# Another order of block 0, totals one step later and later weights of slot 1 in an attention and mixture kernel

## The chip, the cores and the metric

The kernel runs on one core of a Trainium2 chip. The metric is the device time of one execution in microseconds, lower being better, and the number compared is the median of several executions. The core has five engines with a queue each: TensorE (PE in the rows, its weight loads PEld), VectorE (DVE), ScalarE (ACT), GpSimd (POOL) and SyncE (SP). An engine works its queue off in order; engines wait for one another through semaphores.

## The reference

Three layers follow one another, all in float32.

1. Attention with decay over 4 batches, 8 heads, 768 positions, 48 values a head: `y[t] = r[t] · (state + (u k[t]) v[t]ᵀ)`, then `state = w[t] state + k[t] v[t]ᵀ`.
2. A dense layer on the 3072 tokens of width 384: `h = x @ w_in`, `g = max(h, 0) + alpha * min(h, 0)`, `x = g @ w_out`, with 2048 hidden values.
3. Eight experts of 1024 hidden values. Each token goes to the one whose normalised embedding is nearest: `expert_idx = argmax(xn @ en.T / tau)`, `out = gate * (relu(x @ w1[e]) @ w2[e])`, where gate is the chosen expert's softmax probability.

## The kernel before

Tokens are cut into 24 tiles of 128 and those into 8 blocks of 3 tiles. Products in float32 are made of three single-pass products of high and low parts, so most operands exist as a pair: xh and xl, win0h and win0l, gh and gl. ScalarE writes the high part with a copy that rounds, VectorE subtracts it to get the low one.

For block j the dense layer runs 16 f-steps of 128 hidden values. One step has nine matmuls l1 (L458) into h_ps, ScalarE's m (L468, alpha times h), VectorE's min (L472), ScalarE's gh (L478), VectorE's gl (L483), and two steps later nine matmuls l2 (L493) into o_ps.

Block 0 also has to make the attention of its tiles and of those to come, and to convert w_in and w_out to high and low parts. This is issued from the table PLAN, a list of single-engine pieces written in the order in which they enter the queues. `0D.2` is attention part 0 of tile 2 on VectorE, `2P.2` part 2 on TensorE (transposes of k, L345), `2A.2` its copy on ScalarE (L348). 3P (L356) makes the scores, 4P y, 5P the transposes of y (L414) that 5A and 5D turn into xh and xl; 9P (L372) and 9A carry the state, 8A (L297) measures the decay. `cQ.C` is quarter Q of the conversion of weight slab C. `p0P.G`, `p0A.G`, `p1P.G`, `p1A.G` fold the expert embeddings into w_out: p0P (L247) transposes into PSUM, p0A (L252, L253) copies this to wt, p1P (L261) multiplies, p1A (L268, L269) writes s_wp and wout0h. `l.f`, `m.f`, `n.f`, `h.f`, `d.f` and `o.f` are l1, m, min, gh, gl and l2 of step f, and `w.N` is N warm-up matmuls (L444) whose results are not read. 28 more warm-ups run ahead of PLAN. Most PSUM tiles of the attention and of p0P and p1P come from one pool, ps_a, of three buffers; a piece on TensorE that takes one waits until ScalarE or VectorE has emptied the tile that had it.

Behind PLAN the loop over T walks the f-steps of all blocks; `step(k)` moves background generators forward, up to k yields each, and stops at a yield that says WAIT. route(j) (L514 on) computes expert, gate and position of each token of block j. early_table and early_loads, started when block 6 has been routed, compute which experts the first four slots of 256 tokens have and load their weights and rows: `pump` issues w_load (L779, indirect DMAs to raw buffers; there are four of one kind and two of another), `gather` (L811) fetches rows to xg. last_table, started when block 7 has its carry (L559, the tokens counted so far by expert), computes the other slots. Its first act is totals: two small matmuls (L602, L603) that sum carry over partitions and a copy (L605, s_tot).

Then the loop over U walks the slots. A step f of a slot has nine matmuls l3 (L834), ScalarE's g2h (L838), VectorE's g2l (L839) and, two steps later, l4 (L861) with w1h and w1l. Raw weights become high and low parts by split (L790 on ScalarE, L791 on VectorE), 768 columns at a time; split(0, 4) is the first piece of slot 0's second matrix, which l4 of its step 0 reads. EARLY lists the steps of T at which slot 0's splits and transposes run ahead of U.

Of the kernel before, what the change touches and what calls it, by code (L numbers as in the profile page):

```python
# [42 lines left out]
WAIT, DONE, DONE_T = 1, 2, 3  # L43
# [22 lines left out]
AD = (0, 1, 3, 4, 5)  # L66
WARM0 = 28
WPD = (2, 3)
EARLY = [(0, 0, -5), (0, 1, -5), (0, 2, -4), (0, 3, -3), (1, 0, -1), (1, 1, -1), (0, 4, 0)]
SA = 1  # L70
SB = 2
OOB = 1 << 20
# [6 lines left out]

LOADS = [(0, "w"), (0, "rk"), "id", "v", (0, "n"), "e", (1, "w"), (1, "rk"), (1, "n"), (2, "w"), (2, "rk"), (2, "n"), 0, 1, 2, 3, "u"]  # L80
PLAN = """
0D.0 1D.0 8A.0 6D.0 3P.0 3A.0 0D.1 sD 7P.0 7A.0 w.2 1D.1 2P.0 w.8 2A.0 4P.0 6D.1 w.2 c0.0 7P.1 sA 3P.1 0D.2 w.1 4D.0 c1.0 w.8 3A.1
7A.1 c0.1 5P.0 w.2 7P.2 c0.2 7A.2 4P.1 1D.2 5A.0 w.4 c1.1 6D.2 5D.0 w.7 w.3 w.4 c2.0 3P.2 7D.2 c0.3 4D.1 c2.1 3A.2 5P.1 w.4 5A.1
c3.0 c1.2 p0P.0 8A.1 w.2 c2.2 4P.2 5D.1 p0A.0 c1.3 9P.0 eP w.2 8A.2 4D.2 2P.1 9A.0 eA c3.2 5P.2 c0.4 c3.1 2A.1 w.6 w.6 5A.2 5D.2
l.0 c1.4 9P.1 p1P.0 c2.3 m.0 9A.1 c2.4 p1A.0 0D.3 p0P.1 2P.2 2A.2 p0A.1 n.0 c3.4 c0.6 l.1 c0.5 h.0 c3.3 c1.6 7P.3 d.0 c1.5 l.2
7A.3 o.0 m.1 p1P.1 m.2 2P.3 9P.2 c2.6 c0.8 2A.3 p1A.1 c2.5 p0P.2 n.1 c3.6 1D.3 h.1 c0.7 l.3 9A.2 n.2 c3.5 d.1 6D.3 h.2 c1.8 p0A.2
m.3 l.4 9P.3 n.3 o.1 9A.3 l.5 3P.3 8A.3 c2.8 h.3 c1.7 p1P.2 d.2 c0.9 c2.7 d.3 o.2 3A.3 c0.10 c3.8 0D.4 m.5 m.4 n.4 p0P.3 p1A.2
p0A.3 h.4 o.3 c3.7 7P.4 n.5 c1.10 h.5 d.4 4P.3 l.6 7A.4 c2.10 m.6 c0.12 l.7 4D.3 p1P.3 p1A.3 1D.4 d.5 5P.3 5A.3 c3.10 n.6 o.4 m.7
5D.3 h.6 6D.4 d.6 l.8 n.7 0D.5 o.5 c0.11 h.7 m.8 3P.4 7P.5 3A.4 n.8 h.8 c0.14 l.9 7A.5 c1.12 o.6 2P.4 d.7 8A.4 c1.14 m.9 c1.9 o.7
l.10 2A.4 c2.14 d.8 c2.9 c2.12 n.9 p0P.4 c3.9 p0A.4 l.11 m.10 1D.5 p1P.4 h.9 c1.11 8A.5 c3.12 n.10 p1A.4 d.9 4P.4 o.8 l.12 h.10  # L90
4D.4 6D.5 2P.5 c0.13 m.11 p0P.5 d.10 2A.5 5P.4 n.11 c1.13 m.12 c2.11 p0A.5 c3.11 5A.4 o.9 h.11 n.12 c3.14 5D.4 p1P.5 h.12 d.11
p1A.5 l.13 p0P.6 p0A.6 l.14 d.12 m.13 o.10 3P.5 o.11 n.13 c2.13 c0.15 p1P.6 c1.15 m.14 3A.5 h.13 n.14 d.13 h.14 c3.13 l.15 4P.5
m.15 p1A.6 c2.15 4D.5 d.14 p0P.7 o.12 5P.5 p0A.7 p1P.7 5A.5 p1A.7 c3.15 o.13 5D.5 n.15
"""

AT1 = {1: [0, 4, 8], 2: [0, 4, 8]}
# [8 lines left out]
def idx(ap):  # L105
    return bass.IndirectOffsetOnAxis(ap=ap.bitcast(U32), axis=0)
# [3 lines left out]
def tile_main(ctx, tc, keep, x2d, tbl, att, w_in, w_out, alpha, u_row, u_col, emb, tau, w1, w2, cst, out):  # L110
# [125 lines left out]
    def once(nm, shape, dt=F32):  # L236
        return small(nm, shape, dt, 1)
# [362 lines left out]
    def totals(j, ok):  # L600
        tp = ps_a.tile([128, NE + 1, 1], F32, tag="a", name="tot_ps")
        PE.matmul(out=tp[:, 0:NE, 0], lhsT=oneb, rhs=carry[(j + 1) % 2], start=True, stop=True)  # L602
        PE.matmul(out=tp[:, NE:, 0], lhsT=oneb, rhs=ok, start=True, stop=True)  # L603
        tot = once("tot", [128, NE + 1, 1])
        DVE.tensor_copy(out=tot, in_=tp)  # L605
        return tot
# [89 lines left out]

    def last_table():

        tot = totals(NB - 1, okb)
        yield  # L700
        b = above(tot, thr_blk, "nb")
# [2 lines left out]
        n, cu, first = work[:, 0:4 * NE], work[:, 4 * NE:8 * NE], work[:, 8 * NE:12 * NE + 1]  # L704
# [33 lines left out]
        q, h, o, a = (once(f"t{i}", [128, NS1]) for i in range(1, 5))  # L738
# [20 lines left out]
        w = once("t6", [128, 3])  # L759
# [148 lines left out]
    if True:  # L908
# [117 lines left out]
        def pump(most=8, of=(0, 1)):  # L1026
            for i in of:
                while most and queue[i] and busy[i] < (NSG, 2)[i] and queue[i][0][0] < state["known"]:
                    w_load(*queue[i].pop(0))
                    busy[i] += 1  # L1030
                    most -= 1
# [9 lines left out]
        def early_loads():  # L1041
            while state["placed"] < NB - 2:
                yield WAIT
            pump(2)
            for s in range(len(xg)):
                ids_load(s)
            yield
            for i in (1, 0):
                pump(1, (i,))
            yield  # L1050
            for s in range(len(xg)):
                for t in range(2):
                    gather(s, t)
                yield
                if s == 0:
                    pump()
            for s in range(len(xg), ES):
                ids_load(s)

# [14 lines left out]
        for T in range(16 * NB + 2):  # L1074
# [35 lines left out]
            if 32 <= T < 32 + NTILE:  # L1110
                SP.dma_start(out=out[(T - 32) * CH:(T - 31) * CH, :], in_=zero)
            for fn, i, at in EARLY:
                if T - 16 * NB == at:
# [6 lines left out]
        def at(U, fn, *a):  # L1120
            act.setdefault(U, []).append((fn, a))

        for s, k in enumerate(KIND):
            U0, before = FIRST[s], KIND[s - 1]
            at(U0 + (3 if k == "S" else 9), o_scale, s)
            if k != "S":
                for i in range(0 if s else 1, 4):
                    at(U0 + i, split, s, 4 + i)
            else:
                for i in range(2):  # L1130
                    at(U0 + i, relu_single, s, i)
            if s and before != "S":
                for n, i in enumerate((4, 5, 6, 7) if k != "S" else (2, 3, 4, 5, 5, 6, 6, 7)):
                    at(U0 - 8 + i, split, s, n)
            elif s:
                for n in range(4):
                    at(U0 - 2 + (n >= SB), late if n >= SA else split, s, n)
            if s:
                X = U0 - 4 if before != "S" else U0 - 2
                for t in range(NTOK[s]):  # L1140
                    at(X + t, x_T, s, t)
                if s >= ES:
                    at(X - (7 if s == ES else 9), ids_load, s)
# [322 lines left out]
```

## Time and profile before

| what | value |
|---|---|
| median of three executions | 805.33 us (802.21 to 806.11) |
| profiled execution, its own time | 800.48 us |
| its span, first to last instruction | 798.7 us |
| TensorE busy, weight loads busy | 777.0 us, 735.3 us |
| VectorE, ScalarE, GpSimd busy | 545.3, 409.4, 272.2 us |
| mean granted clock of TensorE | 0.994 |
| warm-up matmuls | 89 |

Busy times are sums over the span. Matmuls overlap in the array, and the profile draws each as long as it is under way, so TensorE's sum says little of how full it is. What an edit is worth is read in the stretch where it lies: block 0 ends at some 110 us, the dense layer at some 555 us, and the slots fill the rest.

### The profile page before, as it was taken

The page shows a single profiled execution, that of the slowest core. Times are in us where ns is not written, and L with a number is a line of the kernel's source. Part 1 is how long each engine was busy: PE and PEld are TensorE (multiplying, and loading weights), DVE is VectorE, ACT ScalarE, POOL GpSimd, SP SyncE. Part 2 cuts the span into 40 slices and gives each one's busy share as a digit, 9 for nine tenths or more (in the row PEclk, how much of TensorE's full clock was granted, in tenths as well). Part 3 has the DMA queues.
Part 4 walks back from the last instruction along what each step waited for, and adds up shares of the span by engine and source line. Part 5 has one row for each costly group of instructions (what it writes and reads, how often), then busy time and mean ns, then how long its engine had stood idle before and what let it go on. Part 6 is the DMA issues. An engine that isn't in the chain of part 4 may idle for free.

```text
span 798.7 us, 18664 instructions
## 1 busy us (share of the span) xinstructions
PE 777.0 (97%) x7635; PEld 735.3 (92%) x7635; DVE 545.3 (68%) x1146; ACT 409.4 (51%) x837; POOL 272.2 (34%) x350
## 2 busy tenths in 40 slices
PE   8999999999999999999999999997999999999996
PEld 5689999999999989999999999997999999999996
DVE  8999868767767666676766763663898646567461
ACT  6798654445345435444434543443656545456551
POOL 3102122242242242142224212153275746466511
PEclk9999999999999999999999999998999999999999
DMA  9664422244346213113122100085586756557600
GB/s 326 220 216 144 151 71 72 101 68 144 123 53 218 85 35 105 69 64 71 70 102 71 70 32 2 30 182 195 182 166 199 260 179 216 156 189 230 214 18 30
DMA packets 29230, 102.40 MB, mean 128 GB/s; under 512 B 5418, under 2 KB 12818, under 8 KB 26832
## 3 DMA queue, kind: packets, MB, share of 16 engines
q1 hardware_dynamic: 17584, 53.85, 21.4%
q0 software_dynamic: 11552, 47.27, 19.5%
q8 instruction: 62, 1.02, 0.7%
q14 instruction: 32, 0.26, 0.1%
HBM read 86.49 MB, written 15.23 MB: 127 GB/s over the span
## 4 chain that ended last, share of the span: by engine, by line
PE 75%; DVE 11%; issue 6%; ACT 3%; POOL 2%; DMA 1%; another core or an unknown queue 1%; SPq 0%; POOLq 0%; ACTq 0%; DVEq 0%
PE h_ps L458 23%; PE o_ps L493 23%; PE o_ps L861 9%; PE h_ps L834 9%; PE a_ps L356 3%; PE y_ps L396 2%; PE y_ps L399 2%; DVE w0l L791 1%; DVE PS L282 1%; DMA stg<-in_w_out 1%; POOL out L901 1%; PE t_ps L414 1%; PE u_ps L372 1%; PE x_ps L820 1%
## 5 line engine op out<-in xcount | busy, mean ns | idle before, releaser
L468 ACT ACTIVATE m<-h_ps,al_sb 128x384 f32<-128x384 f32 x128 | 74.0, 580 | 142.4 <-PE h_ps L458 126.3
L472 DVE TENSOR_TENSOR m<-h_ps,m 128x384 f32<-128x384 f32 x128 | 70.8, 553 | 99.7 <-ACT m L468 98.8
L478 ACT ACTIVATE gh<-m 128x384 fp32r<-128x384 f32 x128 | 67.2, 525 | 109.8 <-DVE m L472 107.8
L483 DVE TENSOR_TENSOR gl<-m,gh 128x384 fp32r<-128x384 f32 x128 | 80.8, 632 | 35.2 <-ACT gh L478 32.7
L364 POOL TENSOR_SCALAR_AFFINE_SELECT A<-A 128x512 f32<-128x512 f32 x48 | 33.1, 713 | 203.7 <-ACT A L363 203.7
L834 PE MATMUL h_ps<-yh,w0h 128*128 128x256 f32 (+2 forms) x264 | 81.2, 307 | 1.0 <-DVE g2l L839 0.7
L838 ACT ACTIVATE g2h<-h_ps 128x256 fp32r<-128x256 f32 (+2 forms) x88 | 35.9, 408 | 85.6 <-PE h_ps L834 76.7
L834 PE MATMUL h_ps<-yl,w0h 128*128 128x256 f32 (+2 forms) x264 | 78.7, 298 | 0.5 <-DVE yl L822 0.5
L834 PE MATMUL h_ps<-yh,w0l 128*128 128x256 f32 (+2 forms) x264 | 78.3, 296 | 0.0
L779 POOL DMA_INDIRECT raw<-in_w,wix x48 | 52.8, 1101 | 72.6 <-DVE w0l L791 35.8
L839 DVE SCALAR_TENSOR_TENSOR g2l<-h_ps,g2h 128x256 fp32r<-128x256 f32 (+2 forms) x88 | 39.8, 453 | 45.7 <-ACT g2h L838 40.9
L493 PE MATMUL o_ps<-wout1h,gh 128*128 128x392 f32 x192 | 66.6, 347 | 4.3 <-ACT gh L478 3.9
L861 PE MATMUL o_ps<-w1l,g2h 128*128 128x384 f32 (+2 forms) x208 | 70.4, 338 | 0.0
L861 PE MATMUL o_ps<-w1h,g2l 128*128 128x384 f32 (+2 forms) x208 | 70.2, 338 | 0.0
L861 PE MATMUL o_ps<-w1h,g2h 128*128 128x384 f32 (+2 forms) x208 | 70.2, 338 | 0.0
L458 PE MATMUL h_ps<-xh,win0h 128*128 128x384 f32 x192 | 68.2, 355 | 0.0
L458 PE MATMUL h_ps<-xh,win1h 128*128 128x384 f32 x192 | 68.2, 355 | 0.0
L493 PE MATMUL o_ps<-wout0h,gh 128*128 128x392 f32 x192 | 65.8, 343 | 0.4 <-ACT gh L478 0.4
L493 PE MATMUL o_ps<-wout1h,gl 128*128 128x392 f32 x192 | 65.9, 343 | 0.3 <-issue 0.3
L493 PE MATMUL o_ps<-wout1l,gh 128*128 128x392 f32 x192 | 65.8, 343 | 0.1
L493 PE MATMUL o_ps<-wout0h,gl 128*128 128x392 f32 x192 | 65.5, 341 | 0.0
L493 PE MATMUL o_ps<-wout0l,gh 128*128 128x392 f32 x192 | 65.2, 340 | 0.0
(305 smaller groups left out, 2134.7 us busy)
## 6 DMA issues: line engine op xcount, KB each, us to landing
ld<-in_att SPq DMA_DIRECT2D x18, 1348.5 KB, 6.1
stg<-in_w_in SPq DMA_DIRECT2D x24, 256.0 KB, 3.9
stg<-in_w_out SPq DMA_DIRECT2D x8, 768.0 KB, 7.6
x2d<-rows SPq DMA_DIRECT2D x24, 194.0 KB, 2.7
out<-zero SPq DMA_DIRECT2D x24, 192.0 KB, 7.2
ld<-in_att SPq DMA_DIRECT2D x5, 512.0 KB, 5.4
ld<-in_att SPq DMA_DIRECT2D x3, 452.5 KB, 5.3
raw<-in_w,wix POOLq DMA_INDIRECT x48
```

What stands on the lines that cost most here:

```text
L364: POOL.affine_select(out=h, in_=h, pattern=[[0, HP], [1, CH]], compare_op=ALU.is_gt, fill=0.0, base=0, channel_multiplier=-1)
L458: PE.matmul(out=h, lhsT=w[:, k, :], rhs=x[:, k, :], start=(n == 0), stop=(n == 3 * KD - 1))
L468: ACT.activation(out=m, in_=h_t[j, f], func=AF.Copy, scale=al_sb[:, f:f + 1])
L472: DVE.tensor_tensor(out=m, in0=h_t.pop((j, f)), in1=m, op=ALU.min)
L478: ACT.activation(out=gh, in_=m_t[j, f], func=AF.Copy)
L483: DVE.tensor_tensor(out=gl, in0=m_t.pop((j, f)), in1=gh.bitcast(F32), op=ALU.subtract)
L493: PE.matmul(out=o_t[j][i], lhsT=g[:, s], rhs=w, start=(f == 0 and n == 0), stop=(f == KF - 1 and n == 2))
L779: POOL.indirect_dma_start(out=t, out_offset=None, in_=src, in_offset=idx(wix[:, h, COL[s]:COL[s] + 1]))
L834: PE.matmul(out=h, lhsT=w[:, k, :], rhs=x[:, k, :], start=(n == 0), stop=(n == 3 * KD - 1))
L838: ACT.activation(out=gh, in_=h, func=AF.Relu)
L839: DVE.scalar_tensor_tensor(out=gl, in0=h, scalar=0.0, in1=gh.bitcast(F32), op0=ALU.max, op1=ALU.subtract)
L861: PE.matmul(out=o2_t[s][t][0:height(s, t)], lhsT=g[:, c], rhs=w, start=(f == 0 and n == 0), stop=(f == KE - 1 and n == 2))
```

## The change

There are four edits.

**PLAN is another order of the same pieces.** Warm-ups go from 61 in 15 places to 80 in 23 places. The table takes too many lines to be read; two of its lines before, and the lines that stand at their place:

```diff
-0D.0 1D.0 8A.0 6D.0 3P.0 3A.0 0D.1 sD 7P.0 7A.0 w.2 1D.1 2P.0 w.8 2A.0 4P.0 6D.1 w.2 c0.0 7P.1 sA 3P.1 0D.2 w.1 4D.0 c1.0 w.8 3A.1
+w.1 0D.0 1D.0 w.6 8A.0 6D.0 0D.1 3P.0 3A.0 sD 1D.1 w.4 w.1 7P.0 7A.0 6D.1 2P.0 4P.0 w.3 2A.0 7P.1 w.4 3P.1 0D.2 w.2 w.3 c0.0 sA
...
-m.3 l.4 9P.3 n.3 o.1 9A.3 l.5 3P.3 8A.3 c2.8 h.3 c1.7 p1P.2 d.2 c0.9 c2.7 d.3 o.2 3A.3 c0.10 c3.8 0D.4 m.5 m.4 n.4 p0P.3 p1A.2
+l.3 c0.7 9P.3 h.2 d.1 m.3 o.1 c1.8 9A.3 c2.8 l.4 6D.3 8A.3 p0A.2 n.3 c1.7 h.3 3P.3 p1P.2 d.2 c0.9 p1A.2 o.2 3A.3 c0.10 d.3 c3.8
```

On ScalarE, from the release of the wprime piece p1A.1 (L268, L269) to the scores' copy of tile 3 (3A.3, L363), the queue before is, with p0A.2 in L252 and L253, m.3 and h.2, h.3 in L468 and L478, 9A.3 in L382, 8A.3 in L297 and c2.8 in L226 to win1h:

```order
L478 ACTIVATE gh<-m 128x384
L252 ACTIVATE wt<-wt_ps_935 128x512
L253 ACTIVATE wt<-wt_ps_936 128x256
L468 ACTIVATE m<-h_ps,al_sb 128x384
L382 ACTIVATE st<-u_ps 48x192 x2
L297 ACTIVATE ld,dev<-ld,wmid 128x4x128
L226 ACTIVATE win1h<-stg 128x3x256
L478 ACTIVATE gh<-m 128x384
L212 ACTIVATE stg<-stg 128x768
```

and of the change, on the same engine:

```order
L478 ACTIVATE gh<-m 128x384
L468 ACTIVATE m<-h_ps,al_sb 128x384
L382 ACTIVATE st<-u_ps 48x192 x2
L226 ACTIVATE win1h<-stg 128x3x256
L297 ACTIVATE ld,dev<-ld,wmid 128x4x128
L252 ACTIVATE wt<-wt_ps_975 128x512
L253 ACTIVATE wt<-wt_ps_976 128x256
L478 ACTIVATE gh<-m 128x384
L212 ACTIVATE stg<-stg 128x768
```

The two copies to wt moved behind m.3, 9A.3, c2.8 and 8A.3.

**last_table waits one step more**, ahead of totals, with all that follows in it:

```diff
     def last_table():
 
+        yield WAIT
         tot = totals(NB - 1, okb)
```

On TensorE, in the slot 0 steps behind block 7, the queue before has the totals between an l4 group and an l3 group:

```order
L861 MATMUL o_ps<-w1h,g2l 128x384
L602 LDWEIGHTS oneb
L602 MATMUL tot_ps<-carry_118,oneb 128x8
L603 LDWEIGHTS oneb
L603 MATMUL tot_ps<-okb,oneb 128x1
L834 MATMUL h_ps<-yh,w0h 128x256
```

and of the change, where every line from L700 on has a number one higher, an l4 group ends in front of the products of route(7), which give each token its place (rk_ps):

```order
L862 MATMUL o_ps<-w1h,g2l 128x384
L569 LDWEIGHTS trib
L569 MATMUL rk_ps<-s_oh,trib 128x24
L571 LDWEIGHTS oneb
L571 MATMUL rk_ps<-s_oh,oneb 128x16
L571 LDWEIGHTS oneb
L571 MATMUL rk_ps<-s_oh,oneb 128x8
L572 LDWEIGHTS oneb
L572 MATMUL rk_ps<-carry_119,oneb 128x24
L602 LDWEIGHTS oneb
L602 MATMUL tot_ps<-carry_118,oneb 128x8
```

The totals stand one l3 and l4 group later, behind the rank products of the same step.

**early_loads issues slot 1's first weights behind the gathers of slots 1 and 2**, one each, instead of both behind the gathers of slot 0:

```diff
             for s in range(len(xg)):
                 for t in range(2):
                     gather(s, t)
+                if s:
+                    pump(1)
                 yield
-                if s == 0:
-                    pump()
```

POOL's queue before, from the first two raw loads of slot 0 to the fourth slot's ids:

```order
L779 DMA raw<-in_w,wix 128x1536 x2
L798 DMA ids<-tbl,idsx 128x2 x3
L779 DMA raw<-in_w,wix 128x1536 x2
L811 DMA xg<-x2d,ids 128x388 x2
L779 DMA raw<-in_w,wix 128x1536 x2
L811 DMA xg<-x2d,ids 128x388 x4
L798 DMA ids<-tbl,idsx 128x2
```

and of the change:

```order
L780 DMA raw<-in_w,wix 128x1536 x2
L799 DMA ids<-tbl,idsx 128x2 x3
L780 DMA raw<-in_w,wix 128x1536 x2
L812 DMA xg<-x2d,ids 128x388 x4
L780 DMA raw<-in_w,wix 128x1536
L812 DMA xg<-x2d,ids 128x388 x2
L780 DMA raw<-in_w,wix 128x1536
L799 DMA ids<-tbl,idsx 128x2
```

The third pair of raw loads moved two and four gathers back.

**split(0, 4) leaves EARLY** and runs in step 0 of U, behind l3 and its g2h and g2l, instead of in T = 128 behind slot 0's transposes and ahead of the copies of o_ps to rows:

```diff
-EARLY = [(0, 0, -5), (0, 1, -5), (0, 2, -4), (0, 3, -3), (1, 0, -1), (1, 1, -1), (0, 4, 0)]
+EARLY = [(0, 0, -5), (0, 1, -5), (0, 2, -4), (0, 3, -3), (1, 0, -1), (1, 1, -1)]
...
-                for i in range(0 if s else 1, 4):
+                for i in range(4):
                     at(U0 + i, split, s, 4 + i)
```

## Rows read from the trace of the kernel before

**Rows 1.** Spans: us from first to last instruction, mean granted TensorE clock.

```profile
core 0: 798.7 us, clock 0.994
```

**Rows 2.** Busy us by engine in stretches of the first 90 us.

```profile
core 0: us, PE busy (x) PEld busy (x) DVE busy (x) ACT busy (x) POOL busy (x), PEclk, DMA share, GB/s
...
10.00:20.00 10.00, 9.42 (x263) 6.12 (x253) 9.76 (x16) 8.30 (x26) 4.05 (x4) 1.00 1.04 399
20.00:30.00 10.00, 8.81 (x133) 5.70 (x132) 9.90 (x13) 7.95 (x16) 2.07 (x2) 1.00 0.43 140
...
40.00:50.00 10.00, 8.33 (x134) 6.88 (x133) 8.76 (x12) 9.40 (x23) 0.50 (x1) 1.00 0.72 261
50.00:60.00 10.00, 10.00 (x126) 9.30 (x125) 9.83 (x15) 9.49 (x20) 1.22 (x2) 1.00 0.53 171
...
80.00:90.00 10.00, 9.76 (x205) 8.97 (x203) 9.85 (x17) 6.57 (x14) 2.59 (x3) 1.00 0.57 192
```

**Rows 3.** Waits of PE, 8 to 113 us: total, times, longest us.

```profile
PE wt_ps L247 <- ACT s_wp L268: 1.3, 1, 1.3
...
PE kt_ps L345 <- ACT s_wp L268: 0.5, 1, 0.5
```

**Rows 4.** Totals: timeline (start, us, instruction, idle before and releaser) and busy us by stretch.

```profile
572.73 0.18 PE L602 MATMUL tot_ps<-carry,oneb 128*128 128x8 bf16 x1 [1.00 <-DVE carry L559]
...
575.29 0.96 DVE L791 TENSOR_TENSOR w1l<-raw,w1h 128x768 fp32r<-128x768 f32 x1 [0.31 <-ACT w1h L790]
...
578.88 0.96 DVE L791 TENSOR_TENSOR w1l<-raw,w1h 128x768 fp32r<-128x768 f32 x1 [0.52 <-ACT w1h L790]
...
579.00:601.00 22.00, 21.70 (x149) 20.33 (x148) 21.07 (x69) 12.83 (x24) 15.13 (x18) 1.00 0.80 169
```

**Rows 5.** End of block 7: timeline of ACT and PE, then busy us by stretch.

```profile
549.98 0.58 ACT L468 ACTIVATE m<-h_ps,al_sb 128x384 f32<-128x384 f32 x1 [5.41 <-remote]
...
551.76 0.69 PE L493 MATMUL o_ps<-wout1h,gh 128*128 128x392 f32 x1 [3.93 <-ACT gh L478]
...
552.00:557.00 5.00, 5.00 (x20) 4.91 (x21) 2.69 (x5) 2.14 (x5) 0.00 (x0) 0.50 0.12 50
557.00:562.00 5.00, 5.00 (x37) 5.00 (x37) 2.59 (x5) 4.52 (x13) 0.95 (x1) 0.96 0.00 0
```

**Rows 6.** Timeline of PE and DVE ahead of l.0.

```profile
31.46 2.38 PE L444 MATMUL idle<-oneb 128*128 128x384 bf16 x12
33.83 0.41 PE L458 MATMUL h_ps<-xh,win0h 128*128 128x384 f32 x1
...
33.05 0.56 DVE L426 TENSOR_TENSOR xl<-t_ps,xh 128x384 fp32r<-128x384 f32 x1 [0.46 <-ACT xh L422]
```

**Rows 7.** Timeline of PE and ACT from l.3 to 3P.3.

```profile
48.59 0.42 PE L458 MATMUL h_ps<-xh,win0h 128*128 128x384 f32 x1
...
54.14 0.34 PE L458 MATMUL h_ps<-xh,win0h 128*128 128x384 f32 x1
...
55.81 1.16 PE L356 MATMUL a_ps<-ld 64*128 64x128 f32 x16
...
54.75 0.51 ACT L478 ACTIVATE gh<-m 128x384 fp32r<-128x384 f32 x1
```

**Rows 8.** Timeline of POOL (weights and gathers) and of ACT (first readers).

```profile
536.61 0.96 POOL L779 DMA_INDIRECT raw<-in_w,wix  x1 [0.30 <-issue]
...
539.14 1.02 POOL L811 DMA_INDIRECT xg<-x2d,ids  x1 [0.30 <-issue]
...
604.69 1.38 POOL L779 DMA_INDIRECT raw<-in_w,wix  x1 [4.82 <-DVE g2l L839]
...
563.94 0.84 ACT L790 ACTIVATE w0h<-raw 128x768 fp32r<-128x768 f32 x1
...
619.83 0.84 ACT L790 ACTIVATE w0h<-raw 128x768 fp32r<-128x768 f32 x1
```

**Rows 9.** Timeline of ACT and PE at slot 0's first g2h and l4.

```profile
557.02 0.38 ACT L838 ACTIVATE g2h<-h_ps 128x256 fp32r<-128x256 f32 x1 [1.42 <-PE h_ps L834]
...
559.20 0.34 PE L861 MATMUL o_ps<-w1h,g2h 128*128 128x384 f32 x1
```

More of the change, by code (lines that the diff above doesn't have):

```diff
@@ L81 @@
 PLAN = """
-0D.0 1D.0 8A.0 6D.0 3P.0 3A.0 0D.1 sD 7P.0 7A.0 w.2 1D.1 2P.0 w.8 2A.0 4P.0 6D.1 w.2 c0.0 7P.1 sA 3P.1 0D.2 w.1 4D.0 c1.0 w.8 3A.1
-7A.1 c0.1 5P.0 w.2 7P.2 c0.2 7A.2 4P.1 1D.2 5A.0 w.4 c1.1 6D.2 5D.0 w.7 w.3 w.4 c2.0 3P.2 7D.2 c0.3 4D.1 c2.1 3A.2 5P.1 w.4 5A.1
-c3.0 c1.2 p0P.0 8A.1 w.2 c2.2 4P.2 5D.1 p0A.0 c1.3 9P.0 eP w.2 8A.2 4D.2 2P.1 9A.0 eA c3.2 5P.2 c0.4 c3.1 2A.1 w.6 w.6 5A.2 5D.2
-l.0 c1.4 9P.1 p1P.0 c2.3 m.0 9A.1 c2.4 p1A.0 0D.3 p0P.1 2P.2 2A.2 p0A.1 n.0 c3.4 c0.6 l.1 c0.5 h.0 c3.3 c1.6 7P.3 d.0 c1.5 l.2
@@ L86 @@
-7A.3 o.0 m.1 p1P.1 m.2 2P.3 9P.2 c2.6 c0.8 2A.3 p1A.1 c2.5 p0P.2 n.1 c3.6 1D.3 h.1 c0.7 l.3 9A.2 n.2 c3.5 d.1 6D.3 h.2 c1.8 p0A.2
-m.3 l.4 9P.3 n.3 o.1 9A.3 l.5 3P.3 8A.3 c2.8 h.3 c1.7 p1P.2 d.2 c0.9 c2.7 d.3 o.2 3A.3 c0.10 c3.8 0D.4 m.5 m.4 n.4 p0P.3 p1A.2
-p0A.3 h.4 o.3 c3.7 7P.4 n.5 c1.10 h.5 d.4 4P.3 l.6 7A.4 c2.10 m.6 c0.12 l.7 4D.3 p1P.3 p1A.3 1D.4 d.5 5P.3 5A.3 c3.10 n.6 o.4 m.7
-5D.3 h.6 6D.4 d.6 l.8 n.7 0D.5 o.5 c0.11 h.7 m.8 3P.4 7P.5 3A.4 n.8 h.8 c0.14 l.9 7A.5 c1.12 o.6 2P.4 d.7 8A.4 c1.14 m.9 c1.9 o.7
@@ L90 @@
[L90 to L93, printed above, removed]
+w.1 0D.0 1D.0 w.6 8A.0 6D.0 0D.1 3P.0 3A.0 sD 1D.1 w.4 w.1 7P.0 7A.0 6D.1 2P.0 4P.0 w.3 2A.0 7P.1 w.4 3P.1 0D.2 w.2 w.3 c0.0 sA
@@ new lines @@
+4D.0 w.6 3A.1 7A.1 c1.0 c0.1 w.8 5P.0 7P.2 7A.2 w.4 w.2 1D.2 c0.2 4P.1 c1.1 5A.0 6D.2 w.7 5D.0 w.2 c0.3 c2.0 3P.2 c2.1 4D.1 7D.2
+w.5 w.2 3A.2 5P.1 c3.0 c1.2 5A.1 8A.1 p0P.0 c2.2 4P.2 5D.1 c1.3 p0A.0 9P.0 w.2 9A.0 eP 4D.2 2P.1 5P.2 8A.2 eA c0.4 c3.2 w.3 c3.1
+w.5 2A.1 5A.2 w.2 5D.2 w.5 w.1 c1.4 c2.3 l.0 9P.1 0D.3 c2.4 p1P.0 m.0 p1A.0 9A.1 p0P.1 n.0 p0A.1 2P.2 c0.6 w.2 c3.4 7P.3 l.1 h.0
+c0.5 7A.3 c3.3 c1.6 l.2 d.0 o.0 2A.2 c1.5 p1P.1 m.2 2P.3 9P.2 m.1 c2.6 n.2 p1A.1 n.1 c0.8 2A.3 c2.5 p0P.2 c3.6 1D.3 h.1 c3.5 9A.2
@@ new lines @@
+l.3 c0.7 9P.3 h.2 d.1 m.3 o.1 c1.8 9A.3 c2.8 l.4 6D.3 8A.3 p0A.2 n.3 c1.7 h.3 3P.3 p1P.2 d.2 c0.9 p1A.2 o.2 3A.3 c0.10 d.3 c3.8
+c2.7 m.4 p0P.3 0D.4 n.4 l.5 m.5 p0A.3 o.3 c3.7 n.5 h.4 h.5 d.4 4P.3 7P.4 l.6 c0.12 c1.10 7A.4 l.7 4D.3 c2.10 m.6 1D.4 p1P.3 5P.3
+5A.3 d.5 p1A.3 o.4 m.7 c3.10 n.6 6D.4 l.8 5D.3 n.7 h.6 d.6 h.7 c0.11 0D.5 m.8 o.5 3P.4 7P.5 n.8 3A.4 c0.14 l.9 h.8 c1.12 o.6 2P.4
+7A.5 d.7 o.7 8A.4 c1.14 c1.9 l.10 c2.12 d.8 c2.14 m.9 p0P.4 n.9 c2.9 c3.9 m.10 p0A.4 2A.4 l.11 1D.5 p1P.4 n.10 h.9 d.9 p1A.4 c3.12
@@ L94 @@
+8A.5 4P.4 o.8 h.10 l.12 m.11 6D.5 2P.5 c0.13 c1.11 4D.4 p0P.5 2A.5 5P.4 c2.11 p0A.5 d.10 n.11 c1.13 5A.4 m.12 n.12 o.9 c3.11 h.12
+c3.14 p1P.5 5D.4 h.11 p1A.5 d.11 l.13 p0P.6 l.14 p0A.6 c0.15 d.12 3P.5 o.10 m.13 n.13 o.11 p1P.6 l.15 3A.5 c1.15 m.14 h.13 c2.13
+n.14 4P.5 h.14 d.13 p1A.6 c2.15 c3.13 m.15 4D.5 p0P.7 n.15 d.14 o.12 5P.5 o.13 p0A.7 5A.5 5D.5 p1P.7 c3.15 p1A.7
 """
```

## The prediction

> **What bounds the kernel now.** I read the total first, then the stretches that the four edits touch, and in each of them the waits. The profiled execution took 800.48 us for a span of 798.7 at a granted clock of 0.994 [rows 1]. TensorE is busy almost throughout, but the first 50 us are not its own: VectorE is busy 9.76 of 10 us from 10 to 20, 9.90 from 20 to 30 and 8.76 from 40 to 50, while the weight loads, of which each matmul has one, fill 6.12, 5.70 and 6.88 [rows 2]. TensorE's largest waits in block 0 are 1.3 and 0.5, both for ScalarE's s_wp [rows 3]. From 50 us on TensorE is busy 10.00 of 10, and the later blocks run on it too, so what block 0 has lost or gained by about 60 us reaches the end nearly one for one; 0.24 is idle once more, from 80 to 90 us [rows 2].
>
> [...] From 579 to 601 us VectorE is busy 21.07 of 22 [rows 4]. [...]
>
> **The change, part by part.**
>
> *The new PLAN.* It holds the same pieces; only warm-ups are added, 61 to 80, of which 78 instead of 61 stand ahead of l.0. Twelve of them took 33.83 − 31.46 = 2.37 us, 0.198 each [rows 6], so 17 more are 3.4 us of TensorE work ahead of l.0. They lie beside VectorE, which hands out x at its own pace: l.0 started at 33.83, right behind xl of tile 2 (33.05, 0.56 long) [rows 6]. Behind the last transpose of x, though, 16 warm-ups stand where 12 stood: 31.46 + 16 × 0.198 = 34.6, so l.0 is some 0.8 late. This does not reach the end by itself, since 2P.2 behind it waited 0.5 and p0P.2 1.3 [rows 3], together 1.8; if that cover were gone, it would cost its 0.8.
>
> What sets l.3 is p0P.2's wait for a PSUM buffer, which ScalarE frees. Before, the last piece to do so was p1A.1; l.3 started at 48.59 [rows 7]. Now 2A.3 comes behind p1A.1 and c0.8 where it stood ahead of p1A.1; up to there ScalarE has the same pieces to finish, and the last of them ends at about the same time. I take l.3 at 48.65, 0.06 late.
>
> Then comes a new wait. Before, p0A.2 (two copies to wt) ran ahead of 9A.3, 8A.3 and c2.8, and 3P.3 came at 55.81, behind l.5 [rows 7]. Now l.5 stands behind 3P.3, so 3P.3 is due l.5's 55.81 − 54.14 = 1.67 earlier: 48.65 + (55.81 − 48.59) − 1.67 = 54.20. But p0A.2, whose PSUM buffers 3P.3 takes, stands behind c2.8 and 8A.3. ScalarE's pieces ahead of h.3 are the same set as before, so p0A.2 ends about where h.3 began, at 54.75 [rows 7]. That is a wait of 0.55; I put its upper end at 0.9, for c2.8 waits for VectorE's half of that slab. Queued behind 3P.3 on TensorE are p1P.2, o.2, p0P.3 and l.5. Of it 0.24 is covered by the idle left at 80 to 90 us. PLAN in sum: 0.06 + 0.55 − 0.24 = about +0.4. The lower end is both waits gone with no new one, −1.8; the upper end is l.0's 0.8 uncovered and the new wait at 0.9, +1.7. I take +0.4, since it is followed from rows of the very pieces, where the ends are extremes of cover.
>
> The 19 warm-ups may also be thought to hold the clock. It is granted at 1.00 from 10 to 60 us although TensorE idled 1.3 at a stretch there [rows 2, 3]; nothing is to be bought back, so I set this at 0. [...]
>
> *Totals a step later.* TensorE's product of totals waited 1.00 for VectorE's carry at 572.73 [rows 4], and the l3 group stood behind it. Now it stands behind the rank products, a step later, so that wait goes. VectorE is late next: it idled 0.31 at 575.29 and 0.52 at 578.88 for ScalarE's w1h and is nearly without gap from there to 601 [rows 4]. The stretch comes forward by no more than that idle, −0.83; the ends are 0 and −1.0. The copy s_tot moves behind L575, and the table comes a step later. The raw loads that wait for it were issued from 604.69 on, after an idle of 4.82, and ScalarE first reads such a raw buffer at 619.83 [rows 8]; issued some 2 to 3 us later they still have over 10 us. Cost 0.
>
> *Second slot's first weights later.* On POOL's queue the two raw loads of slot 1 (the first at 536.61) go behind two and four gathers; at 1.02 and an idle of 0.30 for a gather they go out 2.6 and 5.3 us later [rows 8]. ScalarE reads the first at 563.94 [rows 8], over 20 us on. The gathers go out earlier by as much and wait for nothing new; the set of issues up to the fourth ids load is unchanged, and SP's queue too. Cost 0, unless it moves the stall of [rows 5], below.
>
> *split(0, 4) moved.* ScalarE's 0.84 (as long as w0h in [rows 8]) and VectorE's 0.96 (as w1l in [rows 4]) go from ahead of the copies to rows to behind g2h of f = 0, at 557.02 [rows 9]. There w1h ends at about 557.02 + 0.38 + 0.84 = 558.2 and w1l at 559.2; l4(0, 0) began at 559.20 [rows 9] and reads w1l in its second product. The cover is thin but holds: 0, up to +0.5 without. What it leaves behind at 552 gains nothing, as nine l2 products run there at the lower clock anyway.
>
> Sum: 800.48 + 0.4 − 0.83 = 800.05. The profiled execution lies 805.33 − 800.48 = 4.85 below the median of its runs, so the median would be **804.9**.
>
> **The rivals.**
>
> *The stall at 550 us goes* (faster). Raw loads and gathers are queued without a break up to it; if the two loads of slot 1 between the gathers are what delays ScalarE's m, taking them out returns the 3.93 and the low-clock stretch. There 20 matmuls took 5 us, while 37 fitted into the next 5 [rows 5], so 5 × (1 − 20/37) = 2.3 comes back too: 804.9 − 6.2 = 798.7. Against it: the same bytes leave by the same time, and m's source on TensorE is l1, which stood ahead of products that ran long before.
>
> *Block 0's waits go and no new one comes* (faster, though within 0.5%): −1.8 − 0.83, so 802.7. For it: l.5 and the attention pieces are placed anew. Against it: 3P.3's buffers.
>
> *The warm-ups lie on the path* (slower). If VectorE's products arrive no later than TensorE gets to them, the 17 warm-ups push everything by 3.4, less the 0.58 and 1.19 that TensorE idled from 10 to 30 us [rows 2]; with the new wait at 0.9 and less 0.83 this is +1.7: 807.0. With none of that idle usable it is +3.5, 808.8. It decides when l.0 starts later than 33.83 + 1.8, the waits behind it. For it speaks TensorE's busy share of 8.81 to 9.42 there, against it VectorE's of 9.76 and 9.90 [rows 2]. [...]
>
> *The edits do nothing*: VectorE, the bound in both stretches, gives back the totals' wait, and PLAN's +0.4 is what is left: 805.7.
>
> **How the numbers follow.** My forecast, within 2 us of 804.9, has 0.50; the stall gone 0.12; block 0's waits gone 0.15; warm-ups on the path 0.15; nothing done 0.08. Half a per cent, 4 us, is about what a measurement here can tell from no change: faster is below 801.3, slower above 809.4. Below 801.3 lie the stall's 0.12 and about a half of the block-0 case, with the scatter of the runs (802.21 to 806.11): 0.21. Above 809.4 lie the far part of the warm-up case and a split(0, 4) that misses its cover: 0.10. The rest, 0.69, is the same. The range reaches from 799.0, which takes in the block-0 case with the lower run's 3 us, to 808.8; it leaves out the stall and the worst of the warm-ups.
>
> **What would show it.** l.0 at 34.6; p0P.2's wait still over 1; l.3 within 0.3 of 48.65; a wait of 0.5 to 0.9 ahead of 3P.3, for p0A.2; no wait ahead of the totals; VectorE without gap until 601; ScalarE's m of the last f-step late again and TensorE's clock at 0.50 behind it. I am wrong if l.3 moves by over a microsecond, if the clock stays at its upper level around 552 us, or if l4(0, 0) waits for w1l.

## The result: one per cent slower

The changed kernel took 809.22 us (807.79 to 811.2, six executions), the kernel before 801.44 (794.68 to 806.11, six on the same chip): a ratio of 1.0102, with a 95% interval of 1.007 to 1.0135. The profiled execution took 811.12, its span 809.4 instead of 798.7. I had forecast 804.9 within 799.0 to 808.8, as good as no change. Three more executions of the kernel before have also moved its median from 805.33 to 801.44, so the forecast of −0.4 us stands against a measured +7.8.

Where the time went is read from the start of the same matmul in both traces:

| matmul | before | after | late by |
|---|---|---|---|
| first of l.0 | 33.83 | 36.14 | 2.3 |
| first of l.3 | 48.59 | 49.70 | 1.1 |
| an l2 group at the end of block 0 | 112.31 | 113.63 | 1.3 |
| an l1 group | 234.09 | 235.81 | 1.7 |
| an l2 group | 300.93 | 308.19 | 7.3 |
| first l3 of slot 0 | 554.86 | 562.51 | 7.6 |
| first l3 behind the totals before | 572.79 | 579.41 | 6.6 |
| an l3 of slot 3 | 620.66 | 627.88 | 7.2 |
| an l3 four steps on | 630.35 | 640.24 | 9.9 |

So three places cost: block 0 (1.3 to 1.7), some point near 296 us (5.5), and slot 3 (2.7). One gave: the totals (1.0). Both columns are of one execution each, and these two are 10.7 us apart in span where the medians differ by 7.8. The table tells where time was lost, and its sizes hold to a microsecond or two only: e12 below, the changed kernel once more, is only 0.3 late at 82 us.

**Block 0.** Stretches of the changed kernel (us, busy us and instructions by engine, clock, DMA share, GB/s), to hold against [rows 2]:

```profile
10.00:20.00 10.00, 9.12 (x188) 5.84 (x188) 9.76 (x16) 6.80 (x21) 3.60 (x4) 1.00 1.03 396
20.00:30.00 10.00, 10.00 (x174) 6.41 (x175) 8.03 (x11) 7.85 (x17) 3.22 (x3) 1.00 0.41 130
```

From 20 to 30 us TensorE has no idle left and VectorE, which was the bound with 9.90, is down to 8.03. The timeline (start, us, instruction, idle before and releaser) tells why. First 3P.0 and the first copy of its scores in the kernel before, then the changed kernel:

```profile
8.65 1.16 PE L356 MATMUL a_ps<-ld 64*128 64x128 f32 x16 [0.37 <-DVE ld L307]
...
9.84 1.08 ACT L363 ACTIVATE A<-a_ps 128x512 f32<-128x512 f32 x2 [1.10 <-PE a_ps L356]
...
4.61 5.53 PE L444 MATMUL idle<-oneb 128*128 128x384 bf16 x26
10.07 1.16 PE L356 MATMUL a_ps<-ld 64*128 64x128 f32 x16
...
33.02 3.14 PE L444 MATMUL idle<-oneb 128*128 128x384 bf16 x16
...
11.26 1.08 ACT L363 ACTIVATE A<-a_ps 128x512 f32<-128x512 f32 x2 [2.08 <-PE a_ps L356]
...
18.12 1.09 ACT L363 ACTIVATE A<-a_ps 128x512 f32<-128x512 f32 x2 [1.52 <-PE a_ps L356]
...
22.06 0.96 DVE L214 SCALAR_TENSOR_TENSOR stg<-stg 128x768 int32<-128x768 int32 x1 [1.01 <-ACT stg L212]
...
35.21 0.56 DVE L426 TENSOR_TENSOR xl<-t_ps,xh 128x384 fp32r<-128x384 f32 x1 [0.96 <-ACT xh L422]
```

The seven warm-ups ahead of 3P.0 are not beside anything: they start when the 28 are done and hold 3P.0 until 10.07 (8.65 before). ScalarE waits 2.08 for its scores (1.10 before), later 1.52 for the next tile's, comes late to the conversions behind them, and VectorE waits 1.01 for one of these. The last xl then ends at 35.77, two microseconds later than in [rows 6], with 16 warm-ups still running until 36.1.

**The stop near 296 us.** Stretches of the changed kernel, its timeline, and the row of its instruction queue between 294 and 300 us (packets, MB, share of 16 engines):

```profile
295.00:300.00 5.00, 1.95 (x94) 1.41 (x85) 3.18 (x7) 0.00 (x0) 2.81 (x4) 0.93 0.04 3
300.00:305.00 5.00, 4.41 (x14) 4.27 (x14) 1.18 (x3) 0.62 (x2) 0.52 (x1) 0.50 0.56 129
...
299.30 0.24 PE L399 MATMUL y_ps<-ld,A 128*32 128x48 f32 x1 [3.05 <-issue]
...
300.75 0.68 PE L458 MATMUL h_ps<-xl,win1h 128*128 128x384 f32 x1 [0.59 <-issue]
...
303.76 0.58 ACT L468 ACTIVATE m<-h_ps,al_sb 128x384 f32<-128x384 f32 x1 [9.24 <-PE h_ps L458]
...
q8 instruction: 1, 0.02, 2.9%
```

TensorE stops for 3.05 us ahead of the last of 64 small y matmuls, waiting for nothing that the profile shows ("issue"), and then has a granted clock of 0.50 from 300 to 305 us (1.00 there in the kernel before). In the same 6 us the queue q8 fetches instructions: one transfer of 16 KB, which at 2.9% of 16 engines over 6 us was under way for 2.8 us. I take q8 for TensorE's: it made 62 transfers in the whole execution, and the profile has 15,308 matmuls and weight loads, 247 a transfer, where VectorE, ScalarE and GpSimd have 2,333 instructions together. The slices of that view put its start at 295.65 to 295.80, so its end at about 298.5, just ahead of the restart. The kernel before at the same place in the program:

```profile
295.00:300.00 5.00, 4.26 (x23) 3.46 (x23) 2.85 (x7) 0.87 (x2) 1.65 (x3) 1.00 0.38 26
...
294.07 0.35 PE L399 MATMUL y_ps<-ld,A 128*32 128x48 f32 x16
294.36 0.44 PE L458 MATMUL h_ps<-xh,win1h 128*128 128x384 f32 x1
...
q8 instruction: 1, 0.02, 2.6%
```

It has the same slow fetch, 2.5 us long from 294.2 on, but only as the small matmuls end: of the y matmuls (64 of L399 and 32 of L396 between them) the last one or two were still to start, with l1 and l2 behind them at 0.17 us apiece. TensorE works on. In the changed kernel 26 were still to start.

A slow fetch is the exception. The row of q8 over the whole execution before, then two stretches of the changed kernel, 230 to 236 and 464 to 470 us:

```profile
q8 instruction: 62, 1.02, 0.7%
...
q8 instruction: 1, 0.02, 3.0%
...
q8 instruction: 1, 0.02, 1.0%
```

In the trace before, half of the 62 fetches took up to 1.1 us, and eight took more than 2. The second row is a slow fetch, of 2.9 us, that starts just behind a group of y matmuls. The third is a fetch of 0.95 us that starts as such a group begins, 1.4 us ahead of its end. TensorE stopped at neither. In these traces a stop of 3 us has both, a slow fetch and a start among the small matmuls. Both are not always enough: a fetch of 2.2 us in the trace before starts among y matmuls at 168.7, and there TensorE idles for 0.27 only and goes on while the fetch is under way:

```profile
168.88 0.24 PE L396 MATMUL y_ps<-sbd,ld 128*32 128x96 f32 x1 [0.27 <-issue]
```

**Totals and table.** TensorE's row of the totals, its waits from 562 to 650 us (total, times, longest), and POOL's queue, all of the changed kernel:

```profile
581.65 0.17 PE L602 MATMUL tot_ps<-carry,oneb 128*128 128x8 bf16 x1
...
PE x_ps L821 <- DMA xg<-x2d,ids: 1.9, 2, 1.5
...
614.17 1.39 POOL L780 DMA_INDIRECT raw<-in_w,wix  x1 [7.32 <-DVE g2l L840]
615.86 0.97 POOL L780 DMA_INDIRECT raw<-in_w,wix  x1 [0.30 <-issue]
617.14 0.96 POOL L799 DMA_INDIRECT ids<-tbl,idsx  x1 [0.30 <-issue]
...
624.25 1.08 POOL L812 DMA_INDIRECT xg<-x2d,ids  x1 [3.19 <-PE h_ps L835]
```

The totals wait no more. POOL's idle ahead of the first load that needs the table grew from 4.82 [rows 8] to 7.32, 2.5 us. Behind that load in the queue stand the ids of slot 4 and the gathers of rows that they address, and two transposes of x on TensorE now wait 1.9 us for these, of which one alone waits 1.5.

**What stayed.** At the end of block 7 ScalarE's m is late again, by 4.06 instead of the 5.41 of [rows 5], and the low clock follows (0.50 from 560 to 565 us):

```profile
557.62 0.58 ACT L468 ACTIVATE m<-h_ps,al_sb 128x384 f32<-128x384 f32 x1 [4.06 <-remote]
...
560.00:565.00 5.00, 5.00 (x21) 5.00 (x20) 1.44 (x3) 1.44 (x5) 0.00 (x0) 0.50 0.15 64
```

### The profile page after: what moved, and what is told of

Same layout as the page of the kernel before. It is cut to its first block, busy times and chain, and to the rows that moved or that the text cites. A ratio compares the mean times of both kernels' runs of the same rounds, so it can differ in the third digit from the quotient of the medians.

```text
span 809.4 us, 18702 instructions
## 1 busy us (share of the span) xinstructions
PE 785.2 (97%) x7654; PEld 740.4 (91%) x7654; DVE 544.7 (67%) x1146; ACT 409.7 (51%) x837; POOL 274.1 (34%) x350
## 5 line engine op out<-in xcount | busy, mean ns | idle before, releaser
L468 ACT ACTIVATE m<-h_ps,al_sb 128x384 f32<-128x384 f32 x128 | 74.2, 581 | 142.7 <-PE h_ps L458 130.0
L478 ACT ACTIVATE gh<-m 128x384 fp32r<-128x384 f32 x128 | 67.1, 525 | 108.9 <-DVE m L472 104.8
L458 PE MATMUL h_ps<-xl,win1h 128*128 128x384 f32 x192 | 65.5, 341 | 0.6 <-issue 0.6
L458 PE MATMUL h_ps<-xh,win1l 128*128 128x384 f32 x192 | 65.4, 341 | 0.0
```

Source lines behind the costliest of these rows:

```text
L458: PE.matmul(out=h, lhsT=w[:, k, :], rhs=x[:, k, :], start=(n == 0), stop=(n == 3 * KD - 1))
L468: ACT.activation(out=m, in_=h_t[j, f], func=AF.Copy, scale=al_sb[:, f:f + 1])
L478: ACT.activation(out=gh, in_=m_t[j, f], func=AF.Copy)
```

## The experiments

Each ran beside the kernel before on the same chip. For the first eleven, on three chips, this took 790 us: in their traces the late m near 550 us does not come. For the twelfth, on a fourth chip, it took 801. Why m is late there stays open. Times are compared with the kernel before of the same chip. Places inside the traces of e1 to e11 are held against e3's, by the same matmul in both; e5 to e11 ran on other chips than e3.

### e1: the new PLAN alone

The edit is the new table; the rest is as before.

> The kernel before with the new PLAN alone. The trace of the changed kernel is 1.3 to 1.7 us late at the end of block 0, and 5.6 us more are lost near 295 us, where TensorE stops for 3.2 us in the middle of the small y matmuls and then runs at its lower clock. Theory A, TensorE's instruction stream: the 38 more instructions of the new PLAN shift where the next 16 KB of them is fetched, so the stop near 295 us comes with this edit alone: +6 to +8 us, with the stop in the trace. Rival B, the stop is chance or belongs to another edit: +1 to +2 us and no stop.

Measured: 797.34 against 789.94, ratio 1.0087 (1.0064 to 1.011), +7.4 us. The trace has the stop:

```profile
299.07 0.38 PE L399 MATMUL y_ps<-ld,A 128*32 128x48 f32 x2 [2.94 <-issue]
...
295.00:300.00 5.00, 1.65 (x87) 1.22 (x74) 3.05 (x6) 0.00 (x0) 2.68 (x4) 1.00 0.03 3
300.00:305.00 5.00, 5.00 (x21) 4.96 (x21) 1.60 (x3) 1.03 (x2) 0.51 (x1) 0.66 0.72 121
```

So nearly all of the loss is PLAN's, and the stop comes with it: Theory A. Against e3, whose work up to there is that of before, it is 1.9 us late at 82 us, 2.8 at 270 us and 7.2 behind the stop and its low clock, so the stop cost 4.4. The 0.9 that it lost between 200 and 270 us has no experiment; e5, e9 and e10 do not lose it.

### e2: totals a step later alone

```diff
     def last_table():
 
+        yield WAIT
         tot = totals(NB - 1, okb)
```

> The kernel before with totals a step later alone. Theory A, the late table: TensorE's wait of 1.0 at the totals goes, but the transposes of x of slots 4 and on wait for gathers whose ids come from the table, some 2 to 3.5 us: net +1.5 to +2.5 us, with waits of x_ps for xg near 620 us. Rival B, what the prediction had: -0.8 us and no wait of x_ps.

Measured: 791.08 against 789.94, ratio 1.0016 (1.0006 to 1.0025), +1.1 us. TensorE's waits from 555 to 640 us:

```profile
PE x_ps L821 <- DMA xg<-x2d,ids: 2.0, 2, 1.7
```

The edit by itself is a loss. Theory A holds; the size is a little under its range.

### e3 and e4: slot 1's weights, and split(0, 4)

```diff
+                if s:
+                    pump(1)
                 yield
-                if s == 0:
-                    pump()
```

> The kernel before with slot 1's first raw loads issued later, alone. Theory A: no step waits for them, within 0.5 us of before. Rival B: they take away from the stall near 550 us, where ScalarE waited 5.4 us for m: -2 to -6 us.

```diff
-EARLY = [(0, 0, -5), (0, 1, -5), (0, 2, -4), (0, 3, -3), (1, 0, -1), (1, 1, -1), (0, 4, 0)]
+EARLY = [(0, 0, -5), (0, 1, -5), (0, 2, -4), (0, 3, -3), (1, 0, -1), (1, 1, -1)]
...
-                for i in range(0 if s else 1, 4):
+                for i in range(4):
```

> The kernel before with split(0, 4) behind the first g2h alone. Theory A: its cover holds, 0 to +0.5 us. Rival B: l4(0, 0) waits for w1l, +0.5 to +1.5 us.

Measured: e3 790.04 against 789.94, 1.0005 (0.9995 to 1.0014); e4 790.38, 1.0006 (0.9996 to 1.0015). Neither can be told from no change. In e4's trace l4(0, 0) goes from its first to its second product in 0.18 us, without a wait. The trace has another place for the +0.4. TensorE's wait at the totals from 550 to 570 us, in e4 and then in e3:

```profile
PE tot_ps L602 <- DVE carry L559: 1.2, 1, 1.2
...
PE tot_ps L602 <- DVE carry L559: 0.8, 1, 0.8
```

VectorE hands over its carry later with the split in step 0, and with the totals a step later, as in the changed kernel, nothing waits there. Whether e3's edit could relieve the late m near 550 us was not answered here, since m was not late on that chip; in the changed kernel, which has the edit, it still was.

### e5: the new PLAN with 9 warm-ups ahead of it

```diff
-WARM0 = 28
+WARM0 = 9
```

in e1's kernel, so that TensorE has as many instructions up to the end of PLAN as before, in the new order.

> The new PLAN alone with 9 instead of 28 warm-ups ahead of it, so that TensorE has as many instructions up to the end of PLAN as before. Alone with 28 it cost 7.4 us: by the traces some 1.9 in block 0, 0.8 near 235 us, 4.3 at a stop near 296 us. Theory A, place of the instruction fetch: the stop near 296 us goes, and with 3P.0 no longer behind 19 warm-ups block 0's 1.9 goes too: 0 to +1.5 us against before. Rival B, the new order itself: the stop stays, +4 to +7 us.

Measured: 790.45 against 790.22, ratio 1.0009 (0.9994 to 1.0023). The stop is gone, as Theory A had it. Of block 0's 1.9 only half went: it is still 0.95 us late against e3 at 82 us. The trace shows 3P.0 no longer held up, but l.0 still behind 16 warm-ups:

```profile
8.48 2.08 PE L356 MATMUL a_ps<-ld 64*128 64x128 f32 x16 [2.22 <-DVE ld L307]
...
32.11 3.14 PE L444 MATMUL idle<-oneb 128*128 128x384 bf16 x16
35.23 0.42 PE L458 MATMUL h_ps<-xh,win0h 128*128 128x384 f32 x1
```

### e6: the old PLAN with 38 more instructions

```diff
+        for _ in range(19):
+            z = ps_h.tile([128, 1], F32, tag="h", name="tiny")
+            PE.matmul(out=z, lhsT=oneb, rhs=oneb[:, 0:1], start=True, stop=True)
         for T in range(16 * NB + 2):
```

> The kernel before with 19 matmuls of one column, never read, behind the last piece of PLAN: 38 more TensorE instructions, some 0.6 us of work, PLAN unchanged. Theory A, place of the instruction fetch: the stop near 296 us appears, some 3 us without work and a low clock behind it: +3 to +6 us. Rival B, the new order itself makes the stop: +0.2 to +1 us and no stop.

Measured: 796.93 against 790.22, ratio 1.0077 (1.0057 to 1.0096), +6.7 us. That is more than the +3 to +6 of Theory A, since the small matmuls took 2.17 us where I had 0.6. The stop came:

```profile
110.81 2.17 PE L1076 MATMUL tiny<-oneb 128*128 128x1 bf16 x19
...
299.08 0.53 PE L399 MATMUL y_ps<-ld,A 128*32 128x48 f32 x2 [2.84 <-issue]
...
300.00:305.00 5.00, 5.00 (x22) 4.96 (x22) 1.92 (x3) 1.11 (x2) 0.51 (x1) 0.68 0.76 125
```

Against e3 it is 2.94 us late behind them and 6.97 behind the stop, 4.0 us for the stop. Nothing was re-ordered here. Rival B, that the new order makes it, falls.

### e7 and e8: totals later, table on time

```diff
+        yield WAIT
         tot = totals(NB - 1, okb)
-        yield
         b = above(tot, thr_blk, "nb")
```

in the kernel before (e7), and only the line that goes, the `yield`, in the changed kernel (e8).

> The kernel before with totals a step later, and the yield between totals and the first comparison of the table taken out, so that the table is written in the same step as before. Alone the later totals cost 1.2 us. Theory A, the late table makes x_ps wait for its gathers: without the lateness TensorE's wait at the totals still goes and x_ps waits for nothing, -0.5 to -1.0 us against before. Rival B, the moved product itself costs, or VectorE gives it back: 0 to +1.2 us.

> The changed kernel with that one yield taken out, so that the table comes in the step of before. Theory A: 1.5 to 2.5 us faster than the changed kernel, which was 1.0 per cent slower than before, so +5.5 to +6.5 us against before, and no wait of x_ps for xg. Rival B: as slow as the changed kernel, +8 us.

Measured: e7 789.10 against 790.22, ratio 0.9984 (0.9974 to 0.9993), faster than both kernels; e8 795.94, ratio 1.0069 (1.0049 to 1.0088). POOL's queue in e2, then in e7:

```profile
597.42 1.38 POOL L780 DMA_INDIRECT raw<-in_w,wix  x1 [7.32 <-DVE g2l L840]
...
606.96 1.48 POOL L812 DMA_INDIRECT xg<-x2d,ids  x1 [2.66 <-issue]
...
594.90 1.38 POOL L779 DMA_INDIRECT raw<-in_w,wix  x1 [4.82 <-DVE g2l L839]
...
604.61 1.02 POOL L811 DMA_INDIRECT xg<-x2d,ids  x1 [2.35 <-PE o_ps L861]
```

With the table in the old step the idle is 4.82 again, no x_ps waits, and TensorE's work from 564 us on is 1.0 earlier than in e3. The later product alone is worth a little more than was expected of it (−1.1 us); the step that came with it cost twice that. e8 is +5.7 us, at the lower end of theory A. Its stop of 2.7 us cost only 2.1 instead of the 4.4 of e1, and the clock stayed at 1.00 behind it, where e1 has 0.66:

```profile
298.23 0.20 PE L399 MATMUL y_ps<-ld,A 128*32 128x48 f32 x1 [2.68 <-issue]
...
300.00:305.00 5.00, 5.00 (x32) 4.96 (x31) 3.14 (x5) 2.18 (x4) 0.66 (x1) 1.00 0.88 166
```

### e9: the new PLAN with 61 warm-ups

```diff
-w.1 0D.0 1D.0 w.6 8A.0
+0D.0 1D.0 8A.0
...
-w.5 2A.1 5A.2 w.2 5D.2 w.5 w.1 c1.4
+2A.1 5A.2 5D.2 w.1 c1.4
```

> The new PLAN alone with 19 of its warm-ups taken out: the 7 ahead of 3P.0 and 12 of the 15 between 5P.2 and l.0 (with the 3 of w.3 ahead of them left), so 61 as before and as many TensorE instructions as before. With 9 instead of 28 warm-ups ahead of PLAN block 0 was still 0.9 us late and l.0 came at 35.2. Theory A, the warm-ups lie on TensorE's path and the rest of the order costs nothing: no stop near 296 us, l.0 at 34 or earlier, block 0 within 0.4 us, 0 to +0.4 us against before. Rival B, the order itself delays block 0: l.0 earlier but block 0 still 0.7 to 1.5 us late, +0.7 to +1.5 us.

Measured: 790.67 against 790.23, ratio 1.0006 (0.9996 to 1.0015). There is no stop, and l.0 starts as early as before, now waiting for ScalarE's xh instead of standing behind warm-ups:

```profile
31.23 0.87 PE L444 MATMUL idle<-oneb 128*128 128x384 bf16 x4
33.25 0.44 PE L458 MATMUL h_ps<-xh,win0h 128*128 128x384 f32 x1 [1.15 <-ACT xh L422]
```

At 82 us it is 0.05 ahead of e3. The order of the pieces costs nothing and gives nothing that can be measured; what block 0 lost were the warm-ups. With e5, in which only the hold on 3P.0 is gone, about half of the 1.9 lies with that hold and half with the twelve that e9 also takes from the 16 ahead of l.0.

### e10: the new PLAN and 256 more instructions than before

```diff
+        z = ps_h.tile([128, 109], F32, tag="h", name="tiny")
+        for i in range(109):
+            PE.matmul(out=z[:, i:i + 1], lhsT=oneb, rhs=oneb[:, 0:1], start=True, stop=True)
         for T in range(16 * NB + 2):
```

> The new PLAN alone with 109 one-column matmuls, never read, behind its last piece: with the 38 instructions of the new warm-ups 256 more TensorE instructions than before, which are the 16 KB of one fetch, so every fetch behind falls on the same instruction as before. The new PLAN alone cost 7.4 us. Theory A, place of the instruction fetch: the added work costs 3 to 6 us near 112 us and the stop near 296 us is gone; behind 300 us it is as late as behind 112 us, within 1 us. Rival B, more instructions make the stop, wherever they fall: the stop is there, and it is 4 us later behind 300 us than behind 112 us.

Measured: 795.86 against 790.23, ratio 1.007 (1.0053 to 1.0086). Around the y matmuls, which stand some 6 us later here:

```profile
295.00:300.00 5.00, 5.00 (x129) 4.63 (x129) 3.52 (x6) 1.11 (x2) 4.76 (x5) 1.00 0.04 3
300.00:305.00 5.00, 4.24 (x23) 3.46 (x23) 2.84 (x6) 1.02 (x3) 1.47 (x3) 1.00 0.43 28
```

This is the picture of the kernel before, with as many matmuls (23) in the stretch where the slow fetch falls. Against e3 it is 6.25 late at 119 us and 6.27 at 304 us: 2.0 of it is block 0's, as in e1, and the rest the added work; the stop does not come. More instructions do not make the stop, and neither does the lateness; where they put the 16 KB steps does. By slices of 0.15 us the slow fetch, 2.7 us long here (2.8% of 16 engines from 296 to 302 us), starts 0.19 to 0.34 ahead of the first l1 behind the y matmuls; in the kernel before it starts 0.11 to 0.26 ahead of it. So 256 more instructions move it by one transfer, to within 0.23 us, or 30 instructions at the 7.7 ns that one of the y matmuls or its load takes in the kernel before; the 247 matmuls and loads a transfer counted above agree.

### e11 and e12: all four edits, mended and as they were

e11 is the changed kernel with WARM0 = 9 and the table on time.

> All four edits, with 9 warm-ups ahead of PLAN instead of 28 and the one yield of the table taken out. Theory A, the parts add: +0.7 for the new PLAN with 9 warm-ups, -1.1 for totals on time, 0 to +0.4 for the other two: -0.5 to +0.2 us against before. Rival B, they do not add, since block 0's lateness or a fetch moves something else: +1 us or more.

> The changed kernel itself beside the kernel before on the chip of the other experiments. Theory A, the parts add: 7.4 for PLAN, 1.2 for totals, 0.1 and 0.4 for the other two, together +8 to +9 us, with the stop near 296 us and the waits of x_ps for xg both in its trace. Rival B, the first measurement's 7.8 us came from something else on its chip, where ScalarE's m near 550 us was late too: less than +6 us, or a part that no experiment shows.

Measured: e11 790.23 against 790.23, ratio 1.0 (0.999 to 1.0009), as Theory A had it, with neither the stop nor the waits of x_ps. e12, the changed kernel again, 809.2 against 801.33, ratio 1.0103 (1.0079 to 1.0127), +7.9: the first result, from another set of executions. e12's trace has both:

```profile
298.21 0.31 PE L399 MATMUL y_ps<-ld,A 128*32 128x48 f32 x2 [3.27 <-issue]
...
PE x_ps L821 <- DMA xg<-x2d,ids: 1.9, 2, 1.4
```

The parts measured alone, on chips where m was not late, sum to 7.4 + 1.1 + 0.1 + 0.4 = 9.0, and +7.9 lies just under Theory A's range. The split's 0.4 need not count here, since the wait that grew in e4 is gone. The cost of the stop also differs from trace to trace: 2.1 in e8, 4.4 in e1, and in the two traces of the changed kernel 5.4 and 5.9. How the 7.9 divides is not shown closer than that.

## Why the prediction was wrong, step by step

**The instruction stream had no term.** I counted the 19 warm-ups as work and as a hold on the clock. They are also 38 instructions (19 matmuls and their weight loads), and behind them every later instruction lies 38 places further on in the 16 KB steps in which TensorE's stream is fetched. Near 296 us one slow fetch then starts among the small y matmuls. Shown: 38 more without a new order make the stop (e6), the new order without 38 more does not have it (e5, e9), and 256 more take it away again (e10). All five traces with 38 more have the stop, and none of the other nine. That TensorE ran dry is argued. An estimate from the traces: before, the 96 matmuls from 292.88 to 294.36 us (64 into y_ps from A, 32 from sbd) use up 192 instructions at 7.7 ns each, a fetch of 2.8 us brings 247 (the mean of a transfer) at 11 ns each, and one of 1 us at 4. In the changed kernel the stop ends 0.8 us after the fetch, in e6 0.3 to 0.45. But with the same instructions up to there it comes ahead of the last matmul in the changed kernel and e8 and ahead of the last three in e1 and e12, and at 168.7 us TensorE went on with a slow fetch under way. How the fetch holds TensorE up therefore stays open. So does why this fetch takes 2.5 to 3.0 us in the traces of the kernel before, the changed kernel, e6 and e10, when half of the 62 of the trace before take up to 1.1.

**"They lie beside VectorE" was the mis-sized step of PLAN.** I looked at the warm-ups behind the last transpose (l.0 0.8 late) and not at the seven ahead of 3P.0, which ScalarE and behind it VectorE wait for. l.0 was 2.3 late, block 0 1.3 in this trace and 1.9 in e1, against my +0.4. My slower rival was this, with its deciding point: l.0 later than 35.63 meant that the waits of [rows 3] no longer cover it, and it came at 36.14. The cover of 1.8 was too large as well: e5's l.0 is 1.9 later than e3's, and 0.95 of that came through, so only some 0.9 was covered. The row of VectorE's share from 20 to 30 us, 9.90, had looked like a bound that hides TensorE's work; it is one only as long as TensorE delivers in time. The share of weight loads rose there from 5.70 to 6.41 of ten only, yet TensorE had become the bound of that stretch: it had no idle left, and the others waited for a few of its results.

**The new wait at 3P.3** came with the releaser I had named, p0A.2, at 0.17 instead of 0.55. p0P.2 waited 0.49 instead of over 1. That l.3 was itself 1.1 late is not the reason: in e9, where l.3 is 0.4 ahead of e3's, the two waits are 0.16 and 0.57. Both terms were too large by themselves; why was not tried.

**Totals: the gain was about right, the price of the late table wrong.** The wait went, and e7 gains 1.1 where I had 0.83. But "cost 0" for the step later rested on the first reader of a raw buffer, 15 us on in [rows 8]. Behind the same load stand the ids and gathers of slot 4, and their reader x_ps had no such slack: 2.0 us of waits in e2. Of all that moved with the step I had followed only the nearest DMA.

**Right**: slot 1's weights and split(0, 4) cost nothing that can be measured (e3, e4). The rival that the stall near 550 us goes did not come true: in the changed kernel's trace TensorE still waits 2.63 for gh, where it had waited 3.93.

## What to carry to other kernels

Filler matmuls are free only between the moment when TensorE has nothing and the moment when the next result is due: 19 more of them cost block 0 1.9 us here (e1), and without them it was on time (e9). Count from each result that another engine needs, not from the busy share of that engine. A moved producer is priced at the tightest of all readers down the queue, here x_ps with its 2.0 us of waits (e2). And in a long unrolled stream like this one, added instructions can move a later fetch onto a bad place, as 38 of them did in e6: look for small instructions in a row behind the edit, and for an idle of TensorE that is put down to issue.

## What the runs showed that I had not expected

The 16 KB fetch of instructions near 296 us took 2.5 us in the kernel before, 2.8 in the changed kernel, 3.0 in e6 (3.1% of 16 engines from 294 to 300 us) and 2.7 in e10, although the DMA engines were otherwise all but idle (a share of 0.03 or 0.04 from 295 to 300 us in the changed kernel, e1, e6 and e8). Half of the 62 fetches of the trace before took up to 1.1 us. Whether the slow one costs nothing or over 4 us depends in e6 on 38 instructions issued 180 us earlier. Nineteen matmuls of one column took 2.17 us in e6, 0.114 each, when each wrote a tile of its own in two rotating buffers. In e10, where 109 of them wrote the columns of one tile, they took 0.026 each:

```profile
111.99 2.88 PE L1076 MATMUL tiny<-oneb 128*128 128x1 bf16 x109
```
